# First block of x transposed by the DMA instead of TensorE, in a planned attention and feed-forward kernel

## The chip, the cores and the metric

The kernel runs on one core of one Trainium2 chip. Its time is the device time of one execution in microseconds (us); the kernel before has a median of 278.29 us over 5 runs (278.17 to 278.52).

## What is computed

One token block `x` (2048 tokens of 512 features, bf16) passes through two branches, and a gate per token mixes them. Cut to what matters:

```
g = sigmoid((x * gate_w).sum(-1))              # one number per token
# branch a: 32 heads of 16, four segments of 512 tokens
q, k, v = x @ wq, x @ wk, x @ wv
for s in 4 segments:
    a_dot = softmax(causal(q_s k_s^T / 4)) v_s
    a_mem = phi(q_s) M / (phi(q_s) z + 1e-6)   # memory of earlier segments
    o_s   = sigmoid(beta) * a_mem + (1 - sigmoid(beta)) * a_dot
    M, z += phi(k_s)^T v_s, sum phi(k_s)
a = o @ wo
# branch b
b = (relu(x @ W_gate) * (x @ W_up)) @ W_down   # inner width 1792
out = g * a + (1 - g) * b
```

## The kernel before

The tokens are worked in four segments of 512 (`NSEG`, `L`). For each segment the kernel needs x in two forms. `xT[seg % 3]` has features on the partitions; the projections and the feed-forward matmuls read it. `xn[seg % 2]` has tokens on the partitions; only the token gate reads it (`gate_tasks`, line 420 on VectorE: product with `gate_w` and a sum).

For segments 1 to 3 `xT` is filled straight from DRAM by one DMA transpose on the sync queue (`load_xT`, line 310). For segment 0 it is not. `load_halves` (lines 305 and 306) brings `xn[0]` half by the sync queue and half by the scalar queue. `x0_tasks` then transposes it with 16 TensorE transposes into PSUM (line 487) and four copies from PSUM into `xT[0]` (line 492, two on VectorE and two on ScalarE). Before the data lands, TensorE runs ten matmuls on a tile of zeros (`heat`, line 779). wq comes in halves on both queues, wk on the sync queue, wv on the scalar queue. After them the sync queue carries all the weights of the feed-forward branch (`load_gu`, `load_wd`), `gate_w`, wo, and x of segments 1 and 2. Loads share a small set of completion semaphores in rotation, so a load late in the queue waits for one issued eight loads earlier.

The order on every engine comes from a planner (`Plan`). Each piece of work is a `Task` with an engine, an assumed duration, a key (its wished time) and dependencies; `Plan.run` walks through time and picks, per engine, the ready task with the lowest key. The engines then execute that order as it was written. `SHIFT` adds hand-set amounts to the keys of single tasks by their number. `LANDS` is a table of times at which the planner assumes that each load has landed:

```
got_n[0] = load_halves(xn[0], x[0:L, :], 4, "n0")
got_q = load_halves(wq_sb, A_wq, NC, "q")
got_k = load_cols(nc.sync, wk_sb, A_wk, 0, D, "k")
got_v = load_cols(nc.scalar, wv_sb, A_wv, 0, D, "v")
```

Per segment and group of 8 heads (four groups, `c`) the tasks are: `proj_q` and `proj_k` (matmuls of line 468, copies to `QT` on line 517 and `ktr` on line 532, masked copies `KTe` and `KTo` on lines 535 and 538, and for the memory phi(k) in `pkT`, transposed by DMA into `pK`); `proj_v` (into `Vp`, line 561); `attention` (scores in the row-tiled mode of TensorE on line 578, exponentials on ScalarE on line 598, the causal mask on GpSimd on line 607, probabilities times V in the column-tiled mode on line 620); `normalise` (VectorE, lines 638 to 668); `recall` and `memory` for the memory term. `ffn_tasks` has 14 slices of gate and up matmuls (ScalarE relu on line 737, VectorE product into `hT` on line 743), then four output tiles of down and wo matmuls, scaled on line 765 and stored by the sync queue. All of these share eight PSUM banks.

Of the kernel before, what the change touches and what calls it, by code (L numbers as in the profile page):

```python
# [7 lines left out]
BF16 = mybir.dt.bfloat16  # L8
F32 = mybir.dt.float32
ACT = mybir.ActivationFunctionType  # L10
ALU = mybir.AluOpType

P = 128
S = 2048
D = 512
# [4 lines left out]
L = S // NSEG  # L20
F = 1792
NC = D // P
# [7 lines left out]
RH = 16  # L30

SHIFT = {
    21: -90000, 25: -170000, 29: -240000, 31: 210000, 52: 30000, 55: -10000, 58: -140000,
    74: 40000, 81: 90000, 85: 33000, 87: 80000, 88: -40000, 94: -80000, 115: 80000, 121: 100000,
    145: 130000, 204: -20000, 207: -50000, 210: -20000, 213: -3000, 222: -20000, 227: 270000,
    231: 1500, 234: 15600, 237: 30000, 240: -120000, 243: 11999, 246: 2000, 249: -10000,
    252: -14000, 255: 12999, 261: 28000, 264: -2000, 267: 30000, 270: 15000, 273: 28000,
    276: -10000, 279: 20000, 282: -2000, 300: -120000, 312: 24999, 324: -80000, 339: 80000,
    351: -50000, 354: 60000, 364: -20000, 372: -20000, 377: -50000, 379: 70000, 380: -40000,
    383: -100000, 385: 20000, 398: 10000, 400: 100000, 401: 10000, 404: 16000, 406: -130000,  # L40
    407: -4000, 480: -200000, 481: -190000, 544: 50000, 553: -18000, 556: 6000, 559: -30000,
    562: 2000, 565: -10000, 574: 19000, 583: -20000, 586: -10000, 589: -30000, 592: 9000,
    595: 10000, 598: 27000, 604: 2000, 607: -10000, 610: -4000, 613: -3000, 619: -10000,
    628: 21000, 631: -10000, 637: 29999, 661: 69999, 673: 70000, 686: 180000, 687: 150000,
    688: 100000, 689: -100000, 701: -120000, 704: 140000, 705: 110000, 709: -280000, 714: 15000,
    722: -6000, 727: -60000, 735: 15000, 737: 150000, 748: 8000, 751: -90000, 754: -60000,
    757: -10000, 796: -180000, 800: 90000, 801: 10000, 830: -160000, 831: -20000, 834: 140000,
    869: 30000, 903: 5000, 906: 40000, 909: -3000, 915: -15000, 921: -20000, 924: -10000,
    927: 10000, 930: 30000, 933: 10000, 936: 30000, 942: 30000, 945: -30000, 951: -10000,
    957: -20000, 963: -30000, 969: -20000, 972: 30000, 978: 40000, 984: 24000, 987: 209999,  # L50
    999: 110000, 1011: 60000, 1037: -230000, 1038: 60000, 1039: -260000, 1042: -100000,
    1046: -60000, 1047: 50000, 1052: -40000, 1054: -90000, 1057: 30000, 1062: -80000,
    1067: 56000, 1072: -60000, 1077: -50000, 1082: -70000, 1090: 50000, 1093: -20000,
    1096: 20000, 1134: -30000, 1170: 40000, 1239: 14000, 1242: 90000, 1247: 119999, 1248: 99999,
    1251: 10000, 1254: 60000, 1257: -20000, 1263: -2000, 1266: 20000, 1272: 50000, 1275: 60000,
    1278: 140000, 1284: 50000, 1290: 20000, 1293: -70000, 1296: -30000, 1299: -30000,
    1323: 159999,
}


# [154 lines left out]
def kernel(  # L215
# [15 lines left out]
    nc = tc.nc  # L231
    ctx.enter_context(tc.manual_schedule())
    x = A_x.flatten_outer_dims()
# [5 lines left out]
    plan = Plan()  # L239
# [9 lines left out]
    xT = [sb([P, NC, L], BF16, f"xT{i}") for i in range(3)]  # L249
    xn = [sb([P, 4, D], BF16, f"xn{i}") for i in range(2)]  # L250
    wq_sb = sb([P, NC, D], BF16, "wq_sb")
    wk_sb = sb([P, NC, D], BF16, "wk_sb")
    wv_sb = sb([P, NC, D], BF16, "wv_sb")
# [28 lines left out]
    def bank(slot):  # L282
        return ps[:, slot.i * L:(slot.i + 1) * L]

    def work():
        return plan.one("ps", range(7, -1, -1))


    LANDS = dict(n0=4500, q=5950, k=9300, v=9750, g0=11800, u0=13300, gw=13900, g1=15200, u1=16700,
                 x1=18400, g2=20400, u2=21600, g3=22800, u3=24000, d0=27700, d1=30400, o=31800, n1=33400,  # L290
                 x2=35200)

    def arrival(name):
        return plan.add("in_" + name, 0.0, 0.0, None, lat=LANDS[name])

# [3 lines left out]

    def load_cols(eng, t, ap, c0, c1, name):  # L300
        return load(eng, t[:, :, c0:c1], ap.rearrange("(c p) n -> p c n", p=P)[:, :, c0:c1], name)

    def load_halves(dst, src, k, name):
        src = src.rearrange("(c p) n -> p c n", p=P)
        nc.sync.dma_start(out=dst[:, 0:k // 2], in_=src[:, 0:k // 2])
        nc.scalar.dma_start(out=dst[:, k // 2:k], in_=src[:, k // 2:k])
        return arrival(name)

    def load_xT(seg):
        nc.sync.dma_start_transpose(out=xT[seg % 3][:], in_=x[seg * L:(seg + 1) * L, :])  # L310

    def load_xn(seg):
        nc.sync.dma_start(out=xn[seg % 2][:], in_=x[seg * L:(seg + 1) * L, :].rearrange(
            "(t p) n -> p t n", p=P))

    FP = [(0, 512), (512, 1024), (1024, 1408), (1408, F)]
    got_x, got_n, got_g, got_u = {}, {}, {}, {}

    def load_gu(i):
        got_g[i] = load_cols(nc.sync, wg_sb, B_W_gate, *FP[i], "g%d" % i)  # L320
        got_u[i] = load_cols(nc.sync, wu_sb, B_W_up, *FP[i], "u%d" % i)
# [2 lines left out]
        return load(nc.sync, wd_sb[:, a:b, :],  # L324
                    B_W_down.rearrange("(c p) n -> p c n", p=P)[:, a:b, :], name)

    got_n[0] = load_halves(xn[0], x[0:L, :], 4, "n0")
    got_q = load_halves(wq_sb, A_wq, NC, "q")
    got_k = load_cols(nc.sync, wk_sb, A_wk, 0, D, "k")
    got_v = load_cols(nc.scalar, wv_sb, A_wv, 0, D, "v")  # L330
    nc.scalar.dma_start(out=betab[:], in_=A_beta.partition_broadcast(P))
    load_gu(0)
    nc.sync.dma_start(out=gwb[:], in_=gate_w.partition_broadcast(P))
    got_gw = arrival("gw")
    load_gu(1)
    load_xT(1)
    got_x[1] = [arrival("x1")]
    junk = sb([P, L], BF16, "junk")
# [6 lines left out]
    got_n[1] = arrival("n1")  # L345
    load_xT(2)
    got_x[2] = [arrival("x2")]
    plan.add("SP", 33100, -1e9, None)


    ident = sb([P, P], BF16, "ident")
# [57 lines left out]
    def K(unit, part=0.0):  # L409
        return unit * UNIT + part  # L410
# [51 lines left out]
    def matmuls(key, deps, sl, ops, start=True, stop=True, prev=None, width=L, need=()):  # L462
        n = len(ops)
        for k in range(0, n, GM):
            def emit(k=k):
                for q in range(k, min(k + GM, n)):
                    lhsT, rhs = ops[q]()
                    nc.tensor.matmul(bank(sl)[:, 0:width], lhsT=lhsT, rhs=rhs,  # L468
                                     start=(start and q == 0), stop=(stop and q == n - 1))
            first = prev is None  # L470
            m = min(k + GM, n) - k
            t = plan.add("PE", 215.8 * width / L * m, key - (0 if first else CONT), emit, deps,
                         PEL, need=[sl] + list(need) if first else ())
            if not first:
                t.deps.append((prev, 0.0))
            prev, deps = t, ()
        return prev

    def x0_tasks():
        done = []  # L480
        for c in range(NC):
            sl = work()

            def pe(c=c, sl=sl):
                tp = bank(sl).bitcast(BF16)
                for t in range(4):
                    nc.tensor.transpose(tp[:, t * P:(t + 1) * P], xn[0][:, t, c * P:(c + 1) * P],
                                        ident[:])
            a = plan.add("PE", 240, K(-9), pe, [got_n[0]], PEL, need=[sl])
            cp = nc.scalar.copy if c % 2 else nc.vector.tensor_copy  # L490
            done.append(plan.add(
                "ACT" if c % 2 else "DVE", 430, K(-9), lambda c=c, sl=sl, cp=cp: cp(
                    xT[0][:, c, :], bank(sl).bitcast(BF16)[:, 0:L]),
                [a], DVL, frees=[sl]))
        return done

    def proj_mm(w, c, seg):
        return [lambda ci=ci: (w[:, ci, c * P:(c + 1) * P], xT[seg % 3][:, ci, :])
                for ci in range(NC)]
# [10 lines left out]
    def proj_q(seg, c):  # L510
        u, sl = 4 * seg + c, work()
        i = u % RQ
        key = K(4 * seg + c - 2 - (2 if seg else 0))
        war = [att.get(("pv", u - RQ)), att.get(("recall", u - RQ))]
        a = matmuls(key, got_x[seg] + [got_q] + war, sl, proj_mm(wq_sb, c, seg))
        xread.append(a)
        prj["q", seg, c] = plan.add("DVE", 600, key - RQK, lambda: nc.vector.tensor_copy(  # L517
            QT[i][:], bank(sl)), [a], DVL, frees=[sl])
        if seg:
            es, b = phi_exp(key, sl, a)  # L520
            prj["pq", seg, c] = plan.add("DVE", 665, key + 500, lambda: phi(
                pqT[i][:], QT[i][:], ex1[es.i][:]), [b, prj["q", seg, c]], DVL, frees=[es],
                lock=True)
# [255 lines left out]
            nc.tensor.matmul(bank(warm[k % 8]), lhsT=junk[:, 0:P], rhs=junk[:], start=True,  # L779
                             stop=True)  # L780
    plan.add("PE", 5280, -1e9, heat, lat=0, need=warm, frees=warm)
    got_x[0] = x0_tasks()
    for seg in range(NSEG):
        if seg > 1:
            got_n[seg] = plan.add("SP", 520, KA(4 * seg - 4), lambda seg=seg: load_xn(seg),
# [56 lines left out]
```

The softmax here doesn't subtract the row's maximum and nothing guards it: scores larger than these inputs give would overflow.

## Time and profile before

| | us |
|---|---|
| median of 5 runs | 278.29 |
| lowest and highest | 278.17, 278.52 |
| the profiled execution | 278.5 |
| its span | 276.7 |
| TensorE (PE) busy | 265.8 |
| VectorE (DVE) busy | 207.7 |
| ScalarE (ACT) busy | 195.9 |
| GpSimd (POOL) busy | 87.5 |

The profile is of one execution; its span runs from the first instruction to the last, and the 1.8 us between span and time lie around it. A line of the timeline gives the start, the duration, the engine, the line of the code, the operation, what it writes and reads, how many there are in a row, and in brackets how long the engine had been idle and what ended that. "SPq" and "ACTq" are the issuing queues of the sync engine and of ScalarE: a duration there is that of issuing the transfer, and the time to landing is shown apart. Matmuls are pipelined, so the last of a row is counted at its full latency.

### The profile page before, as it was taken

Reading aid. Unit: us, or ns where it says so; the run is one execution under the profiler, and the core shown is the slowest. Engines: PE = TensorE matmul, PEld = TensorE weight load, DVE = VectorE, ACT = ScalarE, POOL = GpSimd, SP = SyncE. Lnnn points to the kernel's source line nnn. Section 1 sums busy time; section 2 is a strip of 40 time slices with the busy share of each in tenths; the row PEclk is TensorE's granted clock in tenths of the full one; section 3 lists DMA queues with packets and bytes.
Section 4 is the critical chain, followed back from the end, with each engine's and each line's share of the span. In section 5 each row is a group of like instructions: output and inputs, shape, how many; then the busy total and the mean of one; then the engine's idle time right before and its main releaser. Section 6 shows DMA issues by size and latency. Waiting matters only on the chain.

```text
span 276.7 us, 5510 instructions
## 1 busy us (share of the span) xinstructions
PE 265.8 (96%) x2178; PEld 113.4 (41%) x2214; DVE 207.7 (75%) x456; ACT 195.9 (71%) x176; POOL 87.5 (32%) x139
## 2 busy tenths in 40 slices
PE   8999999989999999999999999999999999999995
PEld 4343444333333343444343434343444333444543
DVE  3588989999898869698998778999228785638222
ACT  2299898968897778899996878778846776744100
POOL 5013333432424342534333333333301435230000
PEclk9999999999999999999999999999999999999999
DMA  7999945010411100000001000000000000000001
GB/s 232 328 277 347 260 81 168 5 21 0 96 23 20 22 20 21 19 2 19 4 0 25 17 19 5 19 19 2 0 0 4 19 21 19 21 0 0 2 27 48
DMA packets 27993, 15.46 MB, mean 56 GB/s; under 512 B 15680, under 2 KB 27968, under 8 KB 27968
## 3 DMA queue, kind: packets, MB, share of 16 engines
q1 hardware_dynamic: 26752, 14.06, 19.0%
q10 hardware_dynamic: 1216, 1.06, 1.1%
q8 instruction: 17, 0.28, 0.4%
q14 instruction: 8, 0.07, 0.1%
HBM read 9.86 MB, written 2.10 MB: 43 GB/s over the span
## 4 chain that ended last, share of the span: by engine, by line
PE 78%; DVE 9%; ACT 4%; issue 3%; DMA 3%; ACTq 0%; DVEq 0%
PE ps L468 62%; PE ps L578 8%; PE ps L620 6%; DMA wv_sb<-in_A_wv_dram 3%; PE ps L681 2%; ACT E L598 2%; DVE hT L743 1%; ACT ex L507 1%; DVE ktr L532 1%; DVE T L651 1%; DVE junk L420 1%; DVE QT L517 1%; ACT rgr L737 1%; DVE och L656 1%; ACT Vp L561 0%
## 5 line engine op out<-in xcount | busy, mean ns | idle before, releaser
L598 ACT ACTIVATE E<-ps 128x2048 bf16<-128x2048 f32 x80 | 150.6, 1882 | 31.5 <-PE ps L578 26.6
L607 POOL TENSOR_SCALAR_AFFINE_SELECT E<-E 128x512 bf16<-128x512 bf16 x128 | 83.8, 671 | 157.9 <-ACT E L598 157.9
L743 DVE TENSOR_TENSOR hT<-ps,rgr 128x512 bf16<-128x512 f32 x56 | 38.2, 685 | 29.2 <-PE ps L468 21.3
L468 PE MATMUL ps<-xT,wg_sb 128*128 128x512 bf16 x214 | 56.9, 379 | 1.3 <-issue 0.3
L468 PE MATMUL ps<-xT,wu_sb 128*128 128x512 bf16 x220 | 55.8, 380 | 0.8 <-issue 0.5
L468 PE MATMUL ps<-wd_sb,hT 128*128 128x512 bf16 (+1 forms) x233 | 54.5, 367 | 0.8 <-issue 0.5
L737 ACT ACTIVATE rgr<-ps 128x512 bf16<-128x512 f32 x56 | 32.6, 604 | 16.1 <-PE ps L468 11.5
L651 DVE STREAM_TRANSPOSE T<-ps 128x512 f32<-128x512 f32 x56 | 37.3, 694 | 7.1 <-PE ps L620 5.0
L468 PEld LDWEIGHTS <-hT 128*128 128x128 bf16 x238 | 21.9, 98 | 25.1 <-issue 3.9
L468 PEld LDWEIGHTS <-wg_sb 128*128 128x128 bf16 x224 | 20.6, 98 | 26.5 <-issue 4.7
L468 PEld LDWEIGHTS <-wu_sb 128*128 128x128 bf16 x224 | 20.5, 98 | 26.4 <-issue 4.6
L765 DVE TENSOR_SCALAR osr<-ps,ngcol 128x512 bf16<-128x512 f32 (+1 forms) x17 | 12.0, 709 | 13.8 <-PE ps L468 13.7
L507 ACT ACTIVATE ex<-ps 128x512 bf16<-128x512 f32 x24 | 14.4, 599 | 10.0 <-DVE ktr L532 7.5
L620 PE MATMUL ps<-E,Vp 128*17 128x256 bf16 (+3 forms) x512 | 20.8, 300 | 0.4 <-DVE hT L743 0.4
L656 DVE TENSOR_TENSOR och<-T,cfr 128x512 bf16<-128x512 f32 x28 | 20.6, 736 | 0.4
L578 PE MATMUL ps<-QT,KTe 32*128 32x512 bf16 (+3 forms) x256 | 17.3, 302 | 0.7 <-ACT E L598 0.4
L578 PE MATMUL ps<-QT,KTo 32*128 32x512 bf16 (+3 forms) x256 | 17.1, 299 | 0.5 <-ACT E L598 0.4
L468 PE MATMUL ps<-wv_sb,xT 128*128 128x512 bf16 x62 | 16.7, 380 | 0.7 <-DVE T L651 0.4
L468 PE MATMUL ps<-wo_sb,oT 128*128 128x512 bf16 (+1 forms) x65 | 16.9, 366 | 0.3 <-issue 0.2
L468 PE MATMUL ps<-xT,wk_sb 128*128 128x512 bf16 x57 | 16.6, 380 | 0.4 <-ACT ex L507 0.3
L468 PE MATMUL ps<-xT,wq_sb 128*128 128x512 bf16 x59 | 16.0, 379 | 0.6 <-issue 0.3
L620 PEld LDWEIGHTS <-Vp 128*17 128x17 bf16 x512 | 10.9, 91 | 12.9 <-issue 3.9
(70 smaller groups left out, 189.9 us busy)
## 6 DMA issues: line engine op xcount, KB each, us to landing
out_dram<-osr SPq DMA_DIRECT2D x15, 128.0 KB, 1.7
wd_sb<-in_B_W_down_dram SPq DMA_DIRECT2D x2, 896.0 KB, 9.9
xn<-in_A_x_dram SPq DMA_DIRECT2D x3, 512.0 KB, 3.6
wg_sb<-in_B_W_gate_dram SPq DMA_DIRECT2D x2, 512.0 KB, 9.0
wu_sb<-in_B_W_up_dram SPq DMA_DIRECT2D x2, 512.0 KB, 9.3
wg_sb<-in_B_W_gate_dram SPq DMA_DIRECT2D x2, 384.0 KB, 4.5
wu_sb<-in_B_W_up_dram SPq DMA_DIRECT2D x2, 384.0 KB, 5.1
wk_sb<-in_A_wk_dram SPq DMA_DIRECT2D x1, 512.0 KB, 6.8
```

What stands on the lines that cost most here:

```text
L468: nc.tensor.matmul(bank(sl)[:, 0:width], lhsT=lhsT, rhs=rhs, start=(start and q == 0), stop=(stop and q == n - 1))
L507: return es, plan.add("ACT", 478, key + 500, lambda: nc.scalar.activation(ex1[es.i][:], bank(sl), ACT.Exp), [a], ACL, need=[es], frees=[sl])
L578: nc.tensor.matmul(ps[:, j * L + off:j * L + off + n], lhsT=kt[32 * j:32 * j + 32, kb * P:(kb + 1) * P], rhs=QT[i][32 * j:32 * j + 32, kb ...
L598: nc.scalar.activation(Ef[:, e0 * L:e1 * L], ps[:, e0 * L:e1 * L], ACT.Exp, scale=SCALE),
L607: nc.gpsimd.affine_select(out=m, in_=m, compare_op=ALU.is_ge, fill=0.0, base=0, pattern=[[0, 4], [1, P]], channel_multiplier=-1)
L620: nc.tensor.matmul(bank(sl)[32 * j:32 * j + HW, kb * P:kb * P + w], lhsT=Vp[i][:, kb, 8 * c + 2 * j + r, 0:HW], rhs=E[(NFILL * u + f) % RE ...
L651: done.append(plan.add("DVE", 633, key - RL, lambda r=r, sl=sl: nc.vector.transpose(T[ts.i][:, r], bank(sl)), [a] + done, 60 if r else 0, ...
L656: nc.vector.tensor_tensor(och[ds.i].rearrange("p (q r e) -> p r q e", r=2, e=DH), t()[:, :, :, 0:DH], cfr[cs.i][:, :, :, None].to_broadcas ...
L681: a = plan.add("PE", 216, key + r, lambda r=r, sl=sl: nc.tensor.matmul(bank(sl), lhsT=mbd[i][:, c, r].rearrange("p j e -> p (j e)"), rhs=p ...
L737: r = plan.add("ACT", 478, key - RL, lambda sl=gsl, rs=rs: nc.scalar.activation(rgr[rs.i][:], bank(sl), ACT.Relu), [g], ACL, frees=[gsl])
L743: nc.vector.tensor_tensor(hT[hs1.i][:], bank(sl), rgr[rs.i][:], ALU.mult)),
L765: b = plan.add("DVE", 95 + 1.12 * w, key - RL, lambda: nc.vector.tensor_scalar(osr[os.i][:, 0:w], bank(sl)[:, 0:w], ngcol[:, tt:tt + 1], N ...
```

## The change

The first block of x is now brought by one DMA transpose at the head of the sync queue, straight into `xT[0]`. `x0_tasks`, its transposes and its copies are gone. wq comes in two column halves and wk whole on the scalar queue; wv moves to the sync queue, behind the transpose. `xn[0]`, which the token gate still reads, is loaded whole on the sync queue after the second pair of feed-forward weights. The first two head groups wait for the first half of wq only. The table `LANDS` and the table `SHIFT` have new values, and so the planner lays out a new order on all engines. The values of `SHIFT` are left out below; task numbers are also moved by the tasks that are gone.

```
 SHIFT = {
...
-    LANDS = dict(n0=4500, q=5950, k=9300, v=9750, g0=11800, u0=13300, gw=13900, g1=15200, u1=16700,
-                 x1=18400, g2=20400, u2=21600, g3=22800, u3=24000, d0=27700, d1=30400, o=31800, n1=33400,
-                 x2=35200)
+    LANDS = dict(x0=5600, qa=4500, qb=5500, k=7400, v=9000, g0=10900, u0=12500, gw=13200, g1=14700,
+                 u1=16300, n0=18000, x1=20000, g2=22300, u2=23500, g3=24700, u3=26500, d0=29300,
+                 d1=32000, o=33400, n1=34900, x2=36700)
...
-    def load_halves(dst, src, k, name):
-        src = src.rearrange("(c p) n -> p c n", p=P)
-        nc.sync.dma_start(out=dst[:, 0:k // 2], in_=src[:, 0:k // 2])
-        nc.scalar.dma_start(out=dst[:, k // 2:k], in_=src[:, k // 2:k])
-        return arrival(name)
-
...
-    got_n[0] = load_halves(xn[0], x[0:L, :], 4, "n0")
-    got_q = load_halves(wq_sb, A_wq, NC, "q")
-    got_k = load_cols(nc.sync, wk_sb, A_wk, 0, D, "k")
-    got_v = load_cols(nc.scalar, wv_sb, A_wv, 0, D, "v")
+    load_xT(0)
+    got_x[0] = [arrival("x0")]
+    got_q = [load_cols(nc.scalar, wq_sb, A_wq, 256 * i, 256 * i + 256, "q" + "ab"[i])
+             for i in range(2)]
+    got_k = load_cols(nc.scalar, wk_sb, A_wk, 0, D, "k")
+    got_v = load_cols(nc.sync, wv_sb, A_wv, 0, D, "v")
     nc.scalar.dma_start(out=betab[:], in_=A_beta.partition_broadcast(P))
     load_gu(0)
     nc.sync.dma_start(out=gwb[:], in_=gate_w.partition_broadcast(P))
     got_gw = arrival("gw")
     load_gu(1)
+    load_xn(0)
+    got_n[0] = arrival("n0")
     load_xT(1)
...
-    plan.add("SP", 33100, -1e9, None)
+    plan.add("SP", 34600, -1e9, None)
...
-    def x0_tasks():
-        done = []
-        for c in range(NC):
-            sl = work()
-
-            def pe(c=c, sl=sl):
-                tp = bank(sl).bitcast(BF16)
-                for t in range(4):
-                    nc.tensor.transpose(tp[:, t * P:(t + 1) * P], xn[0][:, t, c * P:(c + 1) * P],
-                                        ident[:])
-            a = plan.add("PE", 240, K(-9), pe, [got_n[0]], PEL, need=[sl])
-            cp = nc.scalar.copy if c % 2 else nc.vector.tensor_copy
-            done.append(plan.add(
-                "ACT" if c % 2 else "DVE", 430, K(-9), lambda c=c, sl=sl, cp=cp: cp(
-                    xT[0][:, c, :], bank(sl).bitcast(BF16)[:, 0:L]),
-                [a], DVL, frees=[sl]))
-        return done
-
...
-        a = matmuls(key, got_x[seg] + [got_q] + war, sl, proj_mm(wq_sb, c, seg))
+        a = matmuls(key, got_x[seg] + [got_q[c // 2]] + war, sl, proj_mm(wq_sb, c, seg))
...
-    got_x[0] = x0_tasks()
```

## The prediction

> **What bounds the kernel now.** I read the busy shares first, then the chain that ended last, then who waited for whom, and last the opening of the timeline for TensorE, ScalarE and the sync queue. A difference within 0.2% (0.56 us) is about what a measurement of this kernel cannot tell from no change.
>
> ```profile
> PE 265.8 (96%) x2178; PEld 113.4 (41%) x2214; DVE 207.7 (75%) x456; ACT 195.9 (71%) x176; POOL 87.5 (32%) x139
> ...
> PE 78%; DVE 9%; ACT 4%; issue 3%; DMA 3%; ACTq 0%; DVEq 0%
> ```
>
> TensorE is busy for 96% of the span and carries 78% of the chain. Its own waits are few; the largest ones:
>
> ```profile
> PE ps L468 <- issue: 1.9, 12, 0.2
> PE ps L779 <- DVE mcol_e L357: 1.3, 1, 1.3
> PE ps L578 <- ACT E L598: 0.7, 2, 0.4
> ```
>
> Time is won only where TensorE has less to do, or where it starts its real work earlier. So the opening decides:
>
> ```profile
> 1.25 4.45 PE L779 MATMUL ps<-junk 128*128 128x512 bf16 x10 [1.25 <-DVE mcol_e L357]
> 5.50 1.85 PE L487 MATMUL ps<-ident,xn 128*128 128x128 bf16 x16
> 7.59 2.32 PE L468 MATMUL ps<-xT,wq_sb 128*128 128x512 bf16 x10 [0.25 <-DVE xT L492]
> 9.75 0.59 PE L468 MATMUL ps<-xT,wk_sb 128*128 128x512 bf16 x2
> 10.43 1.02 PE L468 MATMUL ps<-wv_sb,xT 128*128 128x512 bf16 x4
> ...
> 13.82 0.39 PE L578 MATMUL ps<-QT,KTe 32*128 32x512 bf16 x4
> ```
>
> The warm-up matmuls run to 5.5, the 16 transposes of x to 7.3, and the first projection starts at 7.59. Two rates stand in these lines. Ten warm-up matmuls take 4.45 us, 0.43 us each. The ten wq matmuls of the same 512 columns take 2.32 with the last counted at 0.38, so they start 0.216 apart. The transposes (128 columns) start 0.107 apart, still the slow rate. The clock of TensorE doubled between 7.1 and 7.6, just as the projections began.
>
> The loads:
>
> ```profile
> 0.80 0.45 SPq L305 DMA_DIRECT2D xn<-in_A_x_dram  x1
> ...
> 4.42 0.37 SPq L297 DMA_DIRECT2D wu_sb<-in_B_W_up_dram  x1
> ...
> 10.40 5.64 SPq L310 DMA_TRANSPOSE xT<-in_A_x_dram  x1
> ...
> 69.55 1.94 SPq L310 DMA_TRANSPOSE xT<-in_A_x_dram  x1
> ...
> DMA to landing us min/median/max: 4.0/7.7/8.8
> ```
>
> A DMA transpose of a whole x block holds the sync queue 5.64 us and lands in 7.7 when started at 10.40 among other loads; nearly alone (69.55) it holds the queue 1.94 and lands in 4.0. (The last line is the answer for xT.) By the same view the halves of x landed at 4.1 and 4.4, wq at 6.0, wk at 8.6, wv at 10.4.
>
> **What the Trainium skill says.** "DMA: Bandwidth & Descriptors", section on latency and other measured facts, gives DMA transposes 261 GB/s. The trace agrees: 512 KB in 4.0 us against 128 KB (pK) in 2.4 is 393 KB in 1.6 us, 245 GB/s. The same page, "Issuing engines are not separate DMA queues", says that loads from sync and scalar queues interleave on the same 16 engines, so moving wq and wk to the scalar queue makes no bandwidth; the trace agrees in that two 256 KB halves sent on both queues land within 0.3 us of each other. "TensorE: Matmul & The Clock Gate", "What's actually happening": the clock opens only after a busy window of about 3.4 us, which runs free of the kernel. The doubling near 7.4 fits windows of about 0.6 to 4.0 and 4.0 to 7.4: the first held idle time before 1.25 and opened nothing. "TensorEngine Tiling (Array Packing)", "Key Properties": changing the tiling mode drains TensorE; here 0.10 us pass at each change (wg matmuls due to end at 18.90, the tiled ones start at 19.00).
>
> **The change, part by part.** I compared the instruction orders of both kernels as built.
>
> *Removed:* 16 transposes, their 2 copies on ScalarE (1.07 us) and 2 on VectorE (0.78 us). The copies lie ahead of the first projection and nowhere else on the path. With them goes the stretch from 5.5 to 7.59, 2.1 us, if x^T is there at 5.5.
>
> *Added:* the DMA transpose at 0.80. Lower end: alone it takes 4.0, landing at 4.8. Upper end: contended as at 10.40 it takes 7.7, landing at 8.5. With it compete only 512 KB of wq: 4.0 plus up to 512 KB at 328 GB/s (the best early slice), 1.6 us, gives at most 6.4. The kernel's own table says 5.6; its table for the kernel before is within 0.7 us of the trace (x at 4.5 against 4.4, wq 5.95 against 6.0, wk 9.3 against 8.6). I take 5.7, and a first matmul at 5.8.
>
> *The clock:* from 5.8 to 7.4 the projections would still run at the slow rate: 1.6/0.43 = 3.7 matmuls. The other 6.3 of the ten take 6.3 x 0.216 = 1.36. The ten end at 8.76 against 9.75 now: **1.0 us gained** of the 2.1 removed; the warm-up was going on behind the transposes. If the window ended before 5.8, the ten would end at 5.8 + 2.16 = 7.96, a gain of 1.8.
>
> *Weights:* wk has 1.5 MB ahead of or in it, as before, and wv no longer beside it at first, so it lands between 7.4 (the table) and 8.6; it is wanted at 8.8 and costs nothing, but up to 0.3 if x^T is early. wv now stands on the sync queue behind the transpose, which holds that queue 1.9 to 5.6 us: it is issued between 2.7 and 6.4 instead of 1.85. Bytes in front are the same 1.5 MB; landing 9.0 to 10.4. Six matmuls (1.3 us) stand after the ten, so it is wanted at 10.06: 0 to 0.35 us of wait, on TensorE, with everything behind it in order. Today's waits there: summing 0.216 per matmul plus 0.107 per mode change over the order up to the first probability-times-V matmuls gives 21.24 us, and these start at 29.75, so 29.75 - 7.59 - 21.24 = 0.92 us are idle (wv, the wait for ScalarE's ex). I put 0.5 there after: **0.4 gained**. The new order has the same 21.24 us ahead of that point.
>
> *Natural x later:* 512 KB more traffic (15.46 to 15.98 MB), on the sync queue ahead of x^T 1 and all later weights: 512 KB at about 300 GB/s, 1.7 us later. Its issue waits for wk's landing (semaphores are reused after eight loads), x^T 1's for wv's at about 9 to 10.4. Landings against need: natural x has 4.85 MB up to it, which today's traffic had moved by 17.4, and loads land about a microsecond after: 18.4. VectorE wants it after the first hT, whose wu matmuls end near 17.3 in the new order, and two more KT and two pkT steps: 19.2. Slack 0.8; were it late, VectorE would stand and hT, ktr and QT behind it, with them the score matmuls. x^T 1 lands near 20.0 and is wanted by TensorE after 14.66 us of work, at about 21.8: slack 1.8 (today 18.1 against 19.8). wd, wo and x^T 2 move by 1.6 us, and wd is wanted after 71 us of work. These cost nothing on that cover.
>
> *Re-laid order:* the SHIFT table moves nearly every instruction. TensorE's work is otherwise the same count by kind; mode changes rise from 178 to 180: **0.2 lost**. Idle from the first probability matmuls to the last: the trace shows 273.61 - 7.59 - 260.5 = 5.5 us idle in all, less 0.92, so 4.6; 1.5 of it between 58.5 and 74.2, where VectorE never rests, 0.7 near 209 to 220. An order I can't time could give back some or add as much: I take no difference, bounds plus and minus 1.5. VectorE's work in front of each head group's end, counted instruction by instruction with the durations of the page's groups, is at most 2.2 us more than before and up to 7.6 less, ScalarE's never more, so no engine becomes a new bound. The tail (two half tiles, their copies and stores) is alike.
>
> **Sum:** 1.0 + 0.4 - 0.2 = 1.2 us. The profiled execution took 278.5 (span 276.7 and 1.8 around it): 277.3. The median of the runs shown is 278.29, 0.2 lower, so 277.1; I say **277.2**.
>
> **Rivals.**
> 1. *The clock is no obstacle and the new order also loses less.* The window's phase may differ between runs: if it ends before 5.8, the gain is 1.8 + 0.4 - 0.2, plus up to 0.7 of later idle: 2.0 to 2.7, 275.9. For: the window runs free. Against: five runs agree within 0.35 us and this trace puts the opening at 7.4.
> 2. *The gain dissolves in the order.* Later idle grows by about the 1.2 won: 278.3. For: the two orders share hardly a stretch. Against: saturated TensorE absorbs small delays.
> 3. *x^T is late and the clock opens a window later (slower).* After the warm-up TensorE has nothing until x^T. If the gap grows past about 0.7 us, the window from 4.0 to 7.4 is less busy than the opening one of 0.6 to 4.0 (2.8 of 3.4 us), which did not open the clock. Then it opens near 10.9: matmuls from 6.3 to 10.9 do 4.6/0.43 = 10.7 instead of 21, losing 2.3 us; the effective start is 8.6, 1.0 later than today, less 0.4, plus 0.2: 279.1. It decides from a landing of about 6.2. For: the contended transposes took 7.7 and 8.8. Against: at 0.8 only wq competes. With extra idle of the new order, up to 280.
> 4. *It doesn't do what it says:* excluded by the built order; no transposes are left.
>
> **How the numbers follow.** Forecast (gain 0.6 to 2) 0.46, rival 1 0.14, rival 2 0.15, rival 3, with orders that lose over 1.8 us, 0.25. Faster is forecast and rival 1, 0.60; same 0.15; slower 0.25. The range 275.9 to 279.1 reaches into rivals 1 and 3.
>
> **What would show it.** In the profile after: the transpose of x landing near 5.7; first wq matmul at 5.8; its starts 0.43 apart for three or four, then 0.216; wk without wait; wv wait under 0.4; first score matmuls near 12.0 (13.82 now); first probability matmuls near 28.4 (29.75 now); idle of TensorE after that near 4.6. The forecast is wrong if the first projection starts after 7, if the slow rate lasts past 8, or if the lead at the first probability matmuls is lost before the end.

## The result and the profile after

The kernel after takes **279.19 us** in the median (278.4 to 281.94, 19 runs) against 278.32 (277.86 to 279.1, 37 runs) before: 1.0038 times as long, with an interval of 1.0027 to 1.005. It is slower by 0.9 us, where 1.1 less was forecast. The profiled execution took 279.46, 1.0 us more than the one before (278.5). Of that, 0.8 lie inside the span (277.5 against 276.7), where the profile can show them.

The page after, its busy shares, the early DMA rates and the chain by engine:

```profile
PE 266.4 (96%) x2163; PEld 112.1 (40%) x2198; DVE 207.7 (75%) x454; ACT 195.2 (70%) x174; POOL 87.8 (32%) x139
...
GB/s 204 314 261 319 336 122 113 80 20 5 94 21 38 24 38 19 2 2 0 22 17 23 21 0 40 2 0 2 0 0 4 19 21 19 21 0 0 2 0 76
...
PE 78%; ACT 6%; DVE 6%; issue 4%; DMA 4%; SPq 1%; POOL 0%; ACTq 0%; DVEq 0%
```

TensorE (PE) executes 16 transposes fewer and is busy 0.6 us longer: the same matmuls took longer somewhere. DMA has gone from 3 to 4% of the chain. One of TensorE's waits, and where the chain begins:

```profile
PE ps L458 <- DMA xT<-in_A_x_dram: 0.7, 1, 0.7
```

```profile
0.80 5.59 DMA xT<-in_A_x_dram
```

This wait is new, 0.7 us for the transposing load of x, which landed at 6.39 (0.80 + 5.59). The timeline of TensorE shows what it cost:

```profile
1.25 4.45 PE L751 MATMUL ps<-junk 128*128 128x512 bf16 x10 [1.25 <-DVE mcol_e L347]
6.44 4.04 PE L458 MATMUL ps<-xT,wq_sb 128*128 128x512 bf16 x10 [0.73 <-DMA xT<-in_A_x_dram]
10.31 1.03 PE L458 MATMUL ps<-xT,wk_sb 128*128 128x512 bf16 x4
11.17 0.59 PE L458 MATMUL ps<-xT,wq_sb 128*128 128x512 bf16 x2
11.67 2.10 PE L458 MATMUL ps<-wv_sb,xT 128*128 128x512 bf16 x8
13.70 0.39 PE L550 MATMUL ps<-QT,KTe 32*128 32x512 bf16 x4
...
29.69 1.26 PE L592 MATMUL ps<-E,Vp 128*17 128x512 bf16 x32
```

The first projection starts at 6.44, 1.15 us before the old 7.59. But its ten matmuls take 4.04 us instead of 2.32: the first nine start about 0.43 apart, the rate of the warm-up, and only after the ninth, at 9.80, does the spacing fall to 0.216. So the ten end 0.6 us later than before (10.48 against 9.91). The first probability-times-V matmuls start at 29.69 against 29.75. The head (what comes before that point), which was to win 1.4 us, won 0.06. About 0.85 us were lost after it: from there to the end of the span there are 247.81 us (277.5 - 29.69) against 246.95 (276.7 - 29.75).

These two stretches, up to the first probability-times-V matmuls (below: first PV) and after it, are the yardstick for every run that follows. The clock of TensorE is called shut where matmuls of 512 columns start 0.43 us apart, and open where they start 0.216 apart.

### The profile page after: what moved, and what is told of

The parts are those of the page before. It is cut to its first block, busy times and chain, and to the rows that moved or that the text cites. A ratio compares the mean times of both kernels' runs of the same rounds, so it can differ in the third digit from the quotient of the medians.

```text
span 277.5 us, 5470 instructions
## 1 busy us (share of the span) xinstructions
PE 266.4 (96%) x2163; PEld 112.1 (40%) x2198; DVE 207.7 (75%) x454; ACT 195.2 (70%) x174; POOL 87.8 (32%) x139
## 4 chain that ended last, share of the span: by engine, by line
PE 78%; ACT 6%; DVE 6%; issue 4%; DMA 4%; SPq 1%; POOL 0%; ACTq 0%; DVEq 0%
PE ps L458 62%; PE ps L550 8%; PE ps L592 6%; ACT E L570 3%; DMA xT<-in_A_x_dram 2%; PE ps L653 2%; ACT ex L479 2%; DVE QT L489 1%; DMA ratio<-rcol 1%; SPq L438 1%; DVE hT L715 1%; ACT rgr L709 1%; DVE T L623 1%; DMA rq<-ratio 1%; DVE och L628 1%
## 5 line engine op out<-in xcount | busy, mean ns | idle before, releaser
L458 PE MATMUL ps<-xT,wu_sb 128*128 128x512 bf16 x220 | 56.6, 380 | 0.3 <-issue 0.2
L458 PE MATMUL ps<-wd_sb,hT 128*128 128x512 bf16 (+1 forms) x227 | 52.1, 366 | 1.7 <-issue 1.4
L458 PE MATMUL ps<-xT,wq_sb 128*128 128x512 bf16 x60 | 18.3, 414 | 1.2 <-DMA xT<-in_A_x_dram 0.7
```

Source lines behind the costliest of these rows:

```text
L458: nc.tensor.matmul(bank(sl)[:, 0:width], lhsT=lhsT, rhs=rhs, start=(start and q == 0), stop=(stop and q == n - 1))
```

## The experiments

Two explanations of equal rank stood at the start. In the first, the head is what fails: x comes late, the gap after the warm-up keeps the clock of TensorE shut, and a warm-up that covers the gap brings the forecast's gain. In the second, the new order of the planner loses the time after first PV, whatever the head.

**e1_heat13: the kernel after with a longer warm-up.**

```
-        for k in range(10):
+        for k in range(13):
```

> The changed kernel with 13 warm-up matmuls instead of 10 and nothing else, so that TensorE is busy from 1.25 to about 6.8 and x, which landed at 6.4 in the trace of the changed kernel, is met without a gap. Theory A (the 0.7 us gap between warm-up and projections keeps the clock closed for one more window): the projections start near 6.8, the slow rate ends by about 8 (at most 3 slow matmuls instead of 8), the time falls by about 1.0 to 278.2, and the runs scatter less. Theory B (the opening of the clock does not depend on the gap): the start moves 0.4 later, as many slow matmuls up to the same moment near 9.8 (seven), time 279.2 to 279.6. Theory C (the loads behind the head or the new order make all of the loss): 279.2, no change.

Measured: 278.83 (278.07 to 281.17, 22 runs), ratio to before 1.0014 (1.0003 to 1.0026). Its timeline of TensorE:

```profile
1.25 5.71 PE L751 MATMUL ps<-junk 128*128 128x512 bf16 x13 [1.25 <-DVE mcol_e L347]
6.78 2.35 PE L458 MATMUL ps<-xT,wq_sb 128*128 128x512 bf16 x10
8.96 1.03 PE L458 MATMUL ps<-xT,wk_sb 128*128 128x512 bf16 x4
9.82 0.59 PE L458 MATMUL ps<-xT,wq_sb 128*128 128x512 bf16 x2
11.28 1.90 PE L458 MATMUL ps<-wv_sb,xT 128*128 128x512 bf16 x8 [0.87 <-DMA wv_sb<-in_A_wv_dram]
```

Without the gap the ten projections start 0.216 apart at once, although they start 0.34 us later: with TensorE busy up to their start the clock had opened by then. Three more matmuls, which compute nothing, give back 1.35 us in this profile at the end of the ten (9.13 against 10.48). But 0.87 of it goes into a wait for wv, which lands at 11.3, and first PV comes at 29.11, 0.58 earlier than after. From there to the end it is 247.89 again. The slow matmuls are a real loss, and no more than 0.6 us of it is to be had as long as wv lands there. Why a gap of this size does not always cost so much is taken up after the experiments.

**e2_neworder_oldhead: the new order behind the old head.**

```
-    load_xT(0)
...
+    load_halves(xn[0], x[0:L, :], 4)
+    load_halves(wq_sb, A_wq, NC)
...
+    got_k = load_cols(nc.sync, wk_sb, A_wk, 0, D, "k")
+    got_v = load_cols(nc.scalar, wv_sb, A_wv, 0, D, "v")
...
+                nc.tensor.transpose(tp[:, t * P:(t + 1) * P], xn[0][:, t, c * P:(c + 1) * P],
```

> The order of the changed kernel on all engines, with the head of the kernel before: x natural in halves on both queues, 16 TensorE transposes and four copies ahead of the projections, wq, wk, wv on the queues as before, no second load of natural x. Theory A (head even, new order dearer by about 0.8: 5.2 us idle after the first probability matmuls against 4.6, and two more mode changes): 279.1. Theory B (the new order costs nothing, the head all of it): 278.3. Theory C (the later landings cost it): 278.3.

Measured: 279.37 (278.98 to 279.52, 6 runs), ratio 1.0029 (1.0018 to 1.004). First PV comes at 28.35, 1.3 us earlier than in the kernel after, and still it is not faster: 248.85 us follow. One stop of TensorE in the timeline, and the wait of VectorE (DVE) behind it:

```profile
102.17 1.26 PE L596 MATMUL ps<-E,Vp 128*17 128x512 bf16 x32 [0.93 <-DVE osr L741]
```

```profile
DVE grc L448 <- DMA rq<-ratio: 1.3, 1, 1.3
```

The new order sends two exchanges of gate columns through DRAM back to back on the sync queue. In the issues of that queue this is eight loads of `rq` in one row (the line below), where the kernel before has two rows of four, at 84.53 and 90.67:

```profile
89.86 4.58 SPq L442 DMA_DIRECT2D rq<-ratio  x8
```

That costs 0.93 here and nothing in the kernel after, which waits nowhere for `rq`. Without it 247.9 are left, as in e1.

**e3_oldorder_newhead: the old order behind the new head.** The mirror of e2: the loads of the change, with natural x behind `gate_w`, and the planner's tables of before.

```
-    got_n[0] = load_halves(xn[0], x[0:L, :], 4, "n0")
-    got_q = load_halves(wq_sb, A_wq, NC, "q")
+    load_xT(0)
...
+        wq_half(nc.scalar, i)
```

> The order of the kernel before on all engines, without its transposes and copies, and the new head: x by one DMA transpose first on the sync queue, wq in column halves and wk on the scalar queue, wv on the sync queue; natural x after gate_w, ahead of the second pair of feed-forward weights, since this order reads it from 14.5. Theory A (the new head is even because x comes at 6.4 and the clock stays slow until about 9.8): 278.3, plus up to 0.4 where natural x or wu are late. Theory B (the head itself loses 0.9): 279.2. If the head is a gain of 1 us that the new order then loses: 277.3.

Measured: 280.54 (280.29 to 281.02, 5 runs), ratio 1.0076 (1.0064 to 1.0088). The first projection in its timeline:

```profile
8.03 3.19 PE L475 MATMUL ps<-xT,wq_sb 128*128 128x512 bf16 x10 [2.33 <-DMA xT<-in_A_x_dram]
```

x lands at 8.0, later than in any other profile. The first matmuls run 0.216 apart, and from 9.3 to 12.7 they start 0.43 apart: here the clock had opened and shut again after a gap of 2.33 us. First PV comes at 31.63, and 247.07 follow, close to the 246.95 of before. So the end of the span goes with the order, and the head with the loads.

**e4_oldorder_newhead_heat13: e3 with 13 warm-up matmuls.**

> The kernel of the run before it (order of the kernel before, new head) with 13 warm-up matmuls. Theory A: clock open by 8, 1.0 us less than without, 277.3, which is faster than both kernels. Theory B (the gap does not matter): the same as without or 0.4 more, 278.3 to 278.7.

Measured: 280.5 (279.3 to 281.44, 6 runs), ratio 1.0068 (1.0047 to 1.0088). The ten projections take 2.32 us from 6.93, so the clock was open, in spite of a gap of 1.19 us before them, and nothing is won. The stop is elsewhere in its timeline:

```profile
11.79 1.02 PE L475 MATMUL ps<-wv_sb,xT 128*128 128x512 bf16 x4 [2.11 <-DMA wv_sb<-in_A_wv_dram]
```

The old order wants wv after 12 projection matmuls, the new one after 16. With x by transpose at the head, wv is the next thing late, and the expectation had not counted it. (Of 247.99 us after first PV, 0.64 are one extra wait at 49.4.)

**Three ways to bring wv or x earlier.** e5 puts wq and wk behind the transpose on the sync queue, so that x has almost nothing beside it; e6 puts wv on the scalar queue; both on e1. e7 is e5's head under the old order with 12 warm-up matmuls.

```
e5:
-    got_q = [load_cols(nc.scalar, wq_sb, A_wq, 256 * i, 256 * i + 256, "q" + "ab"[i])
+    got_q = [load_cols(nc.sync, wq_sb, A_wq, 256 * i, 256 * i + 256, "q" + "ab"[i])
...
-    got_k = load_cols(nc.scalar, wk_sb, A_wk, 0, D, "k")
+    got_k = load_cols(nc.sync, wk_sb, A_wk, 0, D, "k")
e6:
-    got_v = load_cols(nc.sync, wv_sb, A_wv, 0, D, "v")
+    got_v = load_cols(nc.scalar, wv_sb, A_wv, 0, D, "v")
```

> The changed kernel with 13 warm-up matmuls, and wq and wk on the sync queue behind the transpose and ahead of wv (x, wq a, wq b, wk, wv, then the rest), so that one queue carries the head in the order of need. Against the run with 13 warm-up matmuls and the queues of the change (x landed at 6.8, wv at 11.2, wait for wv 0.87, 278.83). Theory A (x is late because it shares the engines with wq and wk, and wv because it stands behind the transpose beside them): x lands by 5.5, wq by 6.8, wk by 8.3, wv by 10.0; no wait for wv; 278.0. Theory B (landings depend on the bytes alone): x near 6, wv at 11, 278.8, no change. The clock stays covered in both.

> The changed kernel with 13 warm-up matmuls and wv on the scalar queue behind wk, where it is issued near 2.4 without waiting for the transpose; the first feed-forward weights then follow the transpose on the sync queue and compete with wk and wv. If the place behind the transpose makes wv late: it lands near 10.4 as in the kernel before, wait under 0.2, 278.2. If the competition decides: it lands at 11 or later, because wg and wu now take half of the engines from 3.7 on, and the time is 278.8 or above.

> The order of the kernel before, with x by one DMA transpose and wq, wk, wv, wg, wu, gate_w, natural x behind it on the sync queue in this order, and 12 warm-up matmuls. With the new head on two queues this order took 280.5: x landed at 6.9 to 8.0, wv at 11.2 to 11.8 and it wants wv 2.6 us after its start. If one queue brings x by 5.5 and wv by 10.0: start at 6.5, 0.9 of wait for wv, first probability matmuls near 29.3, 277.9, a gain. If landings depend on bytes alone: wv at 11, wait of 1.9, 278.9 or more; natural x late (needed at 14.5) would add up to 0.7.

Measured: e5 279.52 (278.66 to 279.91, 6 runs), ratio 1.0036 (1.0023 to 1.0049); e6 278.76 (278.43 to 279.79, 13 runs), 1.0019 (1.0011 to 1.0027); e7 280.89 (280.64 to 281.4, 5 runs), 1.0087 (1.0074 to 1.01). In e5 the wait moves to wk:

```profile
10.87 1.04 PE L458 MATMUL ps<-xT,wk_sb 128*128 128x512 bf16 x4 [1.45 <-DMA wk_sb<-in_A_wk_dram]
```

x landed at 5.9, not by 5.5 as expected. One queue moved 184 GB/s over the first 10 us, against 258 before and 218 after (stretches of the trace from 0 to 10). So keeping the loads in a row costs more than x's being alone brings; the expectation fell. e6 moves wv from 11.3 to 11.1, which changes nothing. e7 waits three times in the head (wq 0.79, wk 1.14, wv 0.90), reaches first PV at 32.69 and then needs 247.01.

**e8_before_kv_halves_heat8 and e14_before_heat8: the kernel before, with a shorter warm-up, with and without halves.** In all heads with natural x in two halves the transposes can start at 4.64, since both halves are there by 4.5, instead of behind the warm-up at 5.5. e8 stops the warm-up at 8, sends wk and wv like wq, one half on each queue, and moves the small load of beta behind `gate_w` on the sync queue; e14 has the shorter warm-up alone.

```
-    got_k = load_cols(nc.sync, wk_sb, A_wk, 0, D, "k")
-    got_v = load_cols(nc.scalar, wv_sb, A_wv, 0, D, "v")
-    nc.scalar.dma_start(out=betab[:], in_=A_beta.partition_broadcast(P))
+    got_k = load_halves(wk_sb, A_wk, NC, "k")
+    got_v = load_halves(wv_sb, A_wv, NC, "v")
...
+    nc.sync.dma_start(out=betab[:], in_=A_beta.partition_broadcast(P))
...
-        for k in range(10):
+        for k in range(8):
```

> The kernel before, with its TensorE transposes, but 8 warm-up matmuls instead of 10 (x landed at 4.4 while the warm-up ran to 5.5), wk and wv in halves on both queues, so that the first feed-forward weights are issued only at 4.4 and do not compete, and beta on the sync queue after gate_w. If the opening of the kernel before is bound by warm-up and then by wv at 10.4: transposes start at 4.7, first projection at 6.7, wv lands at 9.3 and is wanted at 9.4; 0.9 us less, 277.4, faster than both kernels. If wv still lands at 10.4: 278.2, no change.

> The kernel before with 8 warm-up matmuls instead of 10 and nothing else. If the landing of wv bounds its opening: projections start 0.8 earlier, then wait for wv until 10.4 as before; 278.2, no change, and the 0.6 us gained with halves of wk and wv came from the halves. If the warm-up bounds it: 277.6.

Measured: e8 **277.66** (277.37 to 278.2, 9 runs), ratio 0.9975 (0.9965 to 0.9984): faster than both kernels. e14 278.54 (278.06 to 279.57, 12 runs), 1.0013 (1.0001 to 1.0024). The timeline of e8:

```profile
4.64 1.63 PE L487 MATMUL ps<-ident,xn 128*128 128x128 bf16 x16
6.66 2.32 PE L468 MATMUL ps<-xT,wq_sb 128*128 128x512 bf16 x10 [0.39 <-DVE xT L492]
8.81 0.59 PE L468 MATMUL ps<-xT,wk_sb 128*128 128x512 bf16 x2
9.48 1.02 PE L468 MATMUL ps<-wv_sb,xT 128*128 128x512 bf16 x4
```

and the same stretch of e14:

```profile
9.45 0.60 PE L468 MATMUL ps<-xT,wk_sb 128*128 128x512 bf16 x2 [0.40 <-DVE QT L517]
10.48 1.02 PE L468 MATMUL ps<-wv_sb,xT 128*128 128x512 bf16 x4 [0.43 <-DMA wv_sb<-in_A_wv_dram]
```

Both start the projections 0.9 us before the kernel before. e14 then stops for wv and reaches first PV at 29.81, as before (29.75); e8 does not stop and reaches it at 28.81. So wv was the floor of the opening before the change too: an earlier x alone is worth nothing there. The gain of e8 is that of the halves, unless the moved load of beta (8 KB) has a part in it, which no run separates. In the new order the same limit shows in e1: there the change's own aim, an earlier start, works, and wv takes most of it.

**e9_neworder_kv_halves_heat8: e8's head under the new order.**

> The order of the changed kernel with the best head so far: natural x, TensorE transposes, 8 warm-up matmuls, wk and wv in halves on both queues, beta on the sync queue. The same head on the order of the kernel before took 277.66. If the new order costs 0.9 of itself wherever it starts: 278.5. If its cost came from the head it was paired with: 277.7 or less.

Measured: 278.85 (277.93 to 279.21, 21 runs), ratio 1.0013 (1.0006 to 1.002). First PV comes at 28.27, the earliest of all, and 249.13 us follow, with VectorE's wait for `rq` at 2.3. With one head, the new order costs 1.2 us of median (1.1 by the two ratios). That is more than the 0.9 expected: with an earlier start the wait for `rq` comes on top, as in e2.

**e10, e12, e13: is it the transposition, or the other loads?** e10 is e1 with a plain copy of the same 512 KB in place of the transpose; it and e12 leave the transposition out, so they compute the first segment on a wrong x and serve for timing alone. e12 and e13 also hold the feed-forward weights back, behind two 8 KB loads after wv, with the copy and with the transpose.

```
e10 and e12:
-    load_xT(0)
+    nc.sync.dma_start(out=xT[0][:], in_=x[0:L, :].rearrange("(t p) n -> p t n", p=P))
e12 and e13:
+    for i in range(2):
+        spare = sb([P, H], BF16, f"spare{i}")
+        nc.sync.dma_start(out=spare[:], in_=A_beta.partition_broadcast(P))
```

> The changed kernel with 13 warm-up matmuls, and the first DMA transpose replaced by a plain copy of the same 512 KB into the same tile on the same queue. The first segment is thus computed on an x that is not transposed; all else is as in the run with 13 warm-up matmuls (278.83, wv at 11.2, 0.87 of wait). If the transposition itself makes the head's loads slow: x lands near 5, wv near 10.2, no wait for it, first probability matmuls near 28.3, 278.0. If the bytes and the two queues do: wv at 11 or later, 278.8.

> As the run with a plain copy of x in place of the first transpose (the first segment is computed on an x that is not transposed), with two loads of 8 KB behind wv on the sync queue, so that the first feed-forward weights wait for the landing of x and nothing but x, wq, wk and wv shares the engines at first. 13 warm-up matmuls. If the transposition makes the head's loads slow: x near 4.6, wk by 8, wv by 9.8, no waits on TensorE for weights, more than 2.4 MB moved in the first 10 us, first probability matmuls near 28.3. If it is only the sharing of two queues: landings as in its twin with the transposition.

> The twin of the run before it, with the DMA transpose of x as in the change. If the transposition makes the head's loads slow: x near 6.5, wv at 10.8 or later, about 2.2 MB in the first 10 us, first probability matmuls 0.6 to 1.0 later than its twin. If it does not: within 0.3 us of its twin in every landing.

Measured: e10 282.66 (282.55 to 283.76, 5 runs), ratio 1.0162 (1.0145 to 1.018); e12 281.27 (280.38 to 282.08, 4 runs), 1.0105 (1.0071 to 1.0139); e13 280.32 (279.12 to 281.73, 7 runs), 1.007 (1.0047 to 1.0094). The first projections of e12:

```profile
5.85 1.89 PE L461 MATMUL ps<-xT,wq_sb 128*128 128x512 bf16 x8
9.62 0.61 PE L461 MATMUL ps<-xT,wq_sb 128*128 128x512 bf16 x2 [1.88 <-DMA wq_sb<-in_A_wq_dram]
11.69 1.89 PE L461 MATMUL ps<-xT,wk_sb 128*128 128x512 bf16 x4 [1.46 <-DMA wk_sb<-in_A_wk_dram]
```

and of e13, with a line from later:

```profile
6.75 2.32 PE L461 MATMUL ps<-xT,wq_sb 128*128 128x512 bf16 x10
8.91 1.03 PE L461 MATMUL ps<-xT,wk_sb 128*128 128x512 bf16 x4
...
24.08 1.89 PE L461 MATMUL ps<-xT,wq_sb 128*128 128x512 bf16 x4 [2.20 <-DMA xT<-in_A_x_dram]
```

The time from issue (0.80) to landing of the first x, in e12 and then in e13:

```profile
DMA to landing us min/median/max: 4.6/4.6/4.6
```

```profile
DMA to landing us min/median/max: 5.8/5.8/5.8
```

As a plain copy x lands at 5.4, transposed at 6.6, with the same other loads in the program: the transposition costs 1.2 us of landing. By the DMA records of the two traces, its first piece moves at 2.98 instead of 1.92; from there on the 512 KB take about as long, 2.98 us and 2.85 us. Against what I had expected, the transposition does not slow the head's bytes as a whole: 202 GB/s in e12's first 10 us, 211 in e13's. What changes is who gets them. With the copy, the sync queue had its 1 MB (x, wv) landed by 7.6, and the second half of wq on the scalar queue came at 9.6, wk at 11.6. With the transpose wk came at 8.3 and wv at 10.06, and e13's head has no wait at all. Against e1, e13 only holds back the feed-forward weights, and wv lands 1.2 us earlier: it is they, travelling beside it, that bring wv to 11.3 in e1 and 11.7 in the kernel after. Holding these back moves the loss: x^T of segment 1 comes late and TensorE waits 2.20 us for it at 22.

**e11_after_again: the kernel after, a second profile.**

> The changed kernel once more, for a second look at its head. If the landing of x and the moment at which the clock opens vary between runs, x lands anywhere between 6 and 8 and the slow matmuls number anything between none and ten, and the time follows: 278.4 with an open clock, 280 and more where it closes again. If both are fixed: x at 6.4 and eight slow matmuls, 279.4.

Measured: one run, 280.39. The projection in its timeline:

```profile
7.50 4.00 PE L458 MATMUL ps<-xT,wq_sb 128*128 128x512 bf16 x10 [2.47 <-DMA xT<-in_A_x_dram]
```

Of the same program, x landed at 7.5 this time instead of 6.4. The ten warm-up matmuls took 3.77 us instead of 4.45, so the clock had opened during them, at 4.20, and it shut again at 7.62, just after the projections had begun. First PV is at 30.72, 1.0 us later than in the other profile, and the time is 0.9 us longer. The head of this kernel hangs on the landing of one contended load and on when the clock opens; I take that for the reason why its times spread over 3.5 us where those of before spread over 1.2, which two profiles do not prove.

## Why the prediction was wrong

The forecast was 2.0 us too low: 1.3 of it arose before first PV (28.4 predicted, 29.69 measured) and 0.65 after it. Three terms of its sum failed, x's landing, the clock and the new order.

*What bounds the kernel.* Held. Every gain and loss found lies in the opening of TensorE or in its idle time later.

*x lands at 5.7, with "only 512 KB of wq" competing.* **This step failed first**, in its size. x landed at 6.39, and in other profiles of this head at 6.6 to 8.0. The competition was counted rightly: by the DMA records of the trace, when x's last piece had moved (5.91), the scalar queue had moved wq and 0.03 MB of wk, and the sync queue nothing but x. What came true was the working's own upper end, 6.4; the forecast took 5.7, close to the 5.6 of the kernel's table. That table, taken as a second witness, had been right within 0.7 us on plain loads and was 0.8 too early on this transpose. The lower end was too low as well: it took the 4.0 us of a late transpose, and in e5 and e7, where only 0.07 MB of other loads moved beside it at the head, it needed 5.1.

*The clock opens at 7.4 and costs 3.7 slow matmuls.* **Failed**: it opened near 9.95 (between the starts at 9.80 and 10.09, which are 0.29 apart) and cost eight. This was rival 3, with its condition met (landing after about 6.2) by 0.2 us. The forecast carried the opening time over from the kernel before. There, the transposes had kept TensorE busy from the warm-up to 7.2, and the clock opened at 7.14; what was removed was part of the warm-up. Nor is the time fixed: e11, the same program as after, opened at 4.20. Every trace but that of after keeps a record of the granted clock, and its changes lie 3.41 us or a multiple of that apart. Two such windows of e11 (stretch, its length, busy time of each engine, granted clock, busy share of DMA, GB/s):

```profile
4.20:7.62 3.42, 0.95 (x5) 0.39 (x4) 0.00 (x0) 0.14 (x1) 0.26 (x2) 1.00 1.18 247
7.62:11.03 3.41, 3.41 (x9) 1.22 (x8) 0.70 (x2) 0.00 (x0) 0.00 (x0) 0.50 1.08 341
```

After a window in which TensorE was busy for 0.95 us, the next one was granted half the clock, although TensorE worked through it; then the clock opened again. The busy time of the window before sorts the runs. A shut clock stayed shut after 2.47 us (before, 0.31 to 3.72; the prediction had 2.8 for 0.6 to 4.0) and after 2.68 (after, 3.13 to 6.54, counted back from 9.95), and opened after 2.95 (e11, 0.79 to 4.20). An open one shut after 1.51 (e13, 20.37 to 23.78) and stayed open after 1.93 (e4, 7.75 to 11.17). So the gap of 0.73 us cost eight slow matmuls in after because it lay in the window that had still to open the clock. Gaps of 0.74 in e6 and 1.19 in e4 cost none: there the clock had opened before them, at 5.26 and 4.34. In e1 the window from 3.40 to 6.81 had no gap, and the clock opened at its end.

*Idle before first PV falls from 0.92 to 0.5.* Held, and for a poor reason. The start at 6.44, 21.24 us of work and eight matmuls at 0.216 more each (1.7) give 29.4; measured 29.69, so 0.3 idle. wv landed at 11.66, after the predicted 9.0 to 10.4, and was hidden only because the projections ran slowly. e1 brings the wait out as 0.87 us.

The head's balance: predicted first PV 28.4, measured 29.69; 0.64 of it from x, 0.9 from the clock (4.3 slow matmuls more), 0.2 given back by less idle.

*The new order costs 0.2 and no idle.* **Failed**, though inside its bounds of plus and minus 1.5: it put the change in idle time at nothing, because it had no way to time an order. Eight profiles with the new order and no wait for `rq` (after, e1, e5, e6, e10 to e13) need 247.7 to 247.9 us from first PV to the end. The old order needs 247.0 to 247.3 (before, e3, e7, e8, e14; e4, with its extra wait, 248.0). So the new one costs about 0.75 between the means and 0.85 between after and before: the 0.2 of mode changes and 0.65 of idle. By the sum of 0.216 per matmul and 0.107 per mode change along each order, TensorE falls behind its own work by 4.0 us between first PV and its last matmul before, and by 4.6 after (the prediction's 4.6 for before is another count, from the busy time). The old order loses about 1.9 of it between 55 and 70, the new one 0.4 there. It loses 0.9 at 131, 0.5 near 97 and 0.9 between 180 and 187 instead, waiting for VectorE and for ScalarE's `ex`. The largest, in the timelines of TensorE and of VectorE:

```profile
129.83 0.59 PE L458 MATMUL ps<-xT,wu_sb 128*128 128x512 bf16 x2
131.16 0.59 PE L458 MATMUL ps<-xT,wg_sb 128*128 128x512 bf16 x2 [0.73 <-DVE hT L715]
```

```profile
128.74 0.73 DVE L507 TENSOR_SCALAR KTe<-ktr,mcol_e 128x512 bf16<-128x512 bf16 x1
129.39 1.11 DVE L628 TENSOR_TENSOR och<-T,cfr 128x512 bf16<-128x512 f32 x1
130.43 0.68 DVE L715 TENSOR_TENSOR hT<-ps,rgr 128x512 bf16<-128x512 f32 x1
```

VectorE works without a pause there, and the `hT` that frees TensorE's next PSUM bank stands behind `KTe` and `och`. That the same VectorE work placed otherwise costs nothing is what the old order shows; no run here changed that one place, so this line is a reading and not an experiment.

*Natural x later, x^T 1, wk, the tail.* Held: VectorE never waits for `xn`, TensorE's matmuls wait for no load after the first, and wk is in time. e13 shows how thin the cover was: with the weights held back, x^T 1 comes 2.2 us late.

*The rivals.* Rival 3 named 279.1, and 279.19 came, but by another sum. It had the head 1.0 us late less 0.4, plus 0.2 of order; the head came out level with before and the order 0.85 worse. That the number fits is luck. Rival 2, the gain lost in the order, is the other half of the truth. I had held them apart, at 0.25 and 0.15, and both happened.

What stays open is how the 16 engines divide themselves between the two queues. The Trainium skill ("DMA: Bandwidth & Descriptors", "Queues, rings and completion order") says that each engine goes round the queues by packets. e12, where 1 MB on sync had landed by 7.6 while 0.5 MB on scalar needed until 9.6, fits shares that are unequal in bytes: its trace records pieces of 1024 bytes on sync and of 512 for the halves of wq, and in e13 the transposed x comes in pieces of 256. How many pieces make a packet the trace does not show, and no run varied them alone.

## What to carry to other kernels

Work that is taken out of the opening may be part of the warm-up: ask what keeps TensorE busy in its place, and count the projections at the shut rate until a window has been filled nearly whole (2.95 of 3.41 us was enough here, 2.68 was not). The windows do not start with the kernel, so one trace does not fix when the clock opens. Before an input is brought earlier, look for the next one that the order wants; here wv set the opening, and halving wk and wv over both queues was worth more than any way of bringing x. When a change carries a new order with it, measure the order by itself, from a landmark behind the change to the end.

## What the runs showed of the hardware

- The clock changed only at distances of 3.41 us or a multiple (4.20, 7.62 and 11.03 in e11), and by the busy time of the window just past: 2.68 us did not open it (after), 2.95 did (e11); 1.51 shut it (e13), 1.93 did not (e4).
- Gaps of 2.2 to 2.5 us shut it (e3, e11, e13: the eight matmuls after the wait at 24.08 start 0.43 apart), while one of 2.11 in e4, which fell on two windows, did not. The Trainium skill ("TensorE: Matmul & The Clock Gate", "HAM oscillation") warns of gaps over about 3.4 us; here shorter ones did it, and the measurement decides.
- TensorE's transposes take part in the clock: in e2 the 16 take 1.25 us instead of 1.85 because the clock opened among them, at 5.90; in the kernel before they filled, together with the end of the warm-up, the window that ended with the opening at 7.14.
- A 512 KB DMA transpose at the head of an empty sync queue holds that queue 1.41 us, the next one, at 12.00 among other loads, 7.16.
- Heads with x in halves on both queues moved 257 to 267 GB/s over the first 10 us, the transposing heads on two queues 209 to 237, those on one queue 184 and 196 (e5, e7).
- A 512 KB load of x at the head landed 4.6 us after issue as a copy (e12) and 5.8 transposed (e13); with almost nothing beside it the transposed one still took 5.1 (e5, e7), against 4.0 late in the kernel before.
